# A decode kernel with two cached attention layers: value matmuls of the resident pairs emptied out, queries made by rows, a new issue order

## Chip, cores, metric

One core of a Trainium2 chip. The metric is the device time of one execution in microseconds (us); medians of several executions. In the profiles PE is the engine of the matmuls and PEld its loading of weights; DVE, ACT and POOL are the vector, the scalar and the GpSimd engine; SP issues the cache loads, and SPq is its queue. "<-" before a name says what ended a wait, and "issue" stands for a wait on nothing that the profile shows. A difference of about 1 us between two single profiled executions means nothing: 15 executions of the kernel before lie between 568.26 and 571.89 us.

## The reference

A decode step for 8 sequences (batches): attention, MLP, attention, MLP, all with the same weights. Attention reads the last 1024 positions of a cache of keys (K) and values (V), 32 heads of 128, and both layers read the same cache.

```python
def reference(A_x, A_k_cache, A_v_cache, A_wq, A_wo, B_x, B_w1, B_b1, B_w2, B_b2):
    def _A_ref(x, k_cache, v_cache, wq, wo):       # B=8, Sq=1, D=640, Hq=Hkv=32, Dh=128
        W = min(4096, max(256, Sk // 4))           # 1024 of 4096 positions
        q = (x @ wq) ...                           # [B, 32, 1, 128]
        k = k_cache[:, :, Sk - W:, :];  v = v_cache[:, :, Sk - W:, :]
        p = softmax(einsum("bhqd,bhkd->bhqk", q, k) * Dh ** -0.5)
        return einsum("bhqk,bhkd->bhqd", p, v) ... @ wo
    def _B_ref(x, w1, b1, w2, b2):                 # layernorm, 640 -> 1728, gelu, -> 640
        ...
    x = A_x
    x = x + _A_ref(_layernorm(x), A_k_cache, A_v_cache, A_wq, A_wo)
    x = x + _B_ref(_layernorm(x), B_w1, B_b1, B_w2, B_b2)
    x = x + _A_ref(_layernorm(x), ...)             # the same cache once more
    x = x + _B_ref(_layernorm(x), ...)
    return x
```

The attention outputs of this data are so small beside x that the check of the result does not see them. "Correct" therefore says nothing of the work that this change leaves out.

## The kernel before

The cache moves in *units*: K or V of two heads of one batch, 512 KB, in one of 26 buffers (`unit0` to `unit25`). A *job* is 8 pairs of heads of one batch and one layer. Per batch, the pairs 8 to 15 stay on chip between the layers (16 units, K and V), and the pairs 0 to 7 are loaded twice. So 384 unit loads, 64 layer-1 value steps on resident V units, and 26 - 16 = 10 units for everything that streams while a batch is between its layers.

The kernel is written as a list of tasks; the string `ORDER` says in which order they are issued to the engines' queues. Every engine, and the SP queue that issues the loads, then runs its own list in that fixed order.

```python
    def load(which, job, i):                  # SP queue
        s = take()                            # the unit that was given back first
        ...
        nc.sync.dma_start(units[s][:], cache[job.b, h0:h0 + 2, SK - W:, :].rearrange(
            "u (m c) d -> m u (c d)", c=TOK))

    def values(job, i):                       # PE: 16 matmuls per pair
        first = job.o_ps is None
        if first:
            job.o_ps = psO.tile([P, 16], FP32, tag="o_ps", name="o_ps")
        v, a, z = units[job.v[i]], i % 4, i // 4
        for c in range(TOK):
            nc.tensor.matmul(job.o_ps[:, 2 * i:2 * i + 2], lhsT=v[:, c * DH:(c + 1) * DH],
                             rhs=job.p_v[:, a, c, 2 * z:2 * z + 2], start=(first and c == 0),
                             stop=(c == TOK - 1), skip_group_check=True)
        if not job.kept or job.layer == 1:
            free.append(job.v.pop(i))         # the unit may be loaded again

    # chain of one batch between its layers: MLP, layernorm, then the queries
        def queries():                        # heads 16 to 31: 80 matmuls of one column
            ...
                for kc in range(NKC):
                    nc.tensor.matmul(t["q"][:, h:h + 1], lhsT=wq_sb[:, kc, c0:c0 + DH],
                                     rhs=xn[:, kc, 0:1], start=(kc == 0), stop=(kc == NKC - 1))
        def queries_row():                    # heads 0 to 15: 20 matmuls of 512 columns
            ...
```

The softmax here doesn't subtract the row's maximum and nothing guards it: scores larger than these inputs give would overflow.

Of the kernel before, what the change touches and what calls it, by code (L numbers as in the profile page):

```python
# [15 lines left out]
P = 128  # L16
NB = 8
# [20 lines left out]
AHEAD = 4  # L38
PV = 2
BIG = 30000.0  # L40
ORDER = (
    "zH<)K)9HzB%%z@&@1B#{Oz;z@zAz=-#@z9$<#,z4z5z5((z2786z/--zC{4{5${0z,z;z,+z9{(z+z,&${%z5z70z(/z{)&z%z&#"
    "z-z#z.z0zu+zpzpzpz+zoz,%zmz*y~(z(z((y~zf#$z#z#z#z#z%##$*z#zY)*y|zV+*y|ywyxytysyrywyvyqytysysyqyq%ypy"
    "pypzB&yoyozAzCyoyoyoyoyo*yn$(z:ylylylz5ylylz4yl(ykyk&z.ykz<ytz9ykz+ykz(z)#yjz,*yo#ygz($#y{z)$yjyj(yc"
    "&ygygyuygz1yi,ya)y`y`yiyiymyfygylykydyi***ygy]yeyeyvycy]ys&#y^##y^zZyny^yl$y[y[yWykyW$yVyXyXyfyc#ycy"
    "V&y`yTzEyTyZyTyTyTyYyYyYyUyU($#yQz5%yPz3yQz4yP%z1y[yOyZyQyYz+yYySyXz)z(yX&*z$(yUyL(y}y|$yRyOyQyxyQyJ"
    "yQ$#yN$&yL$0yJyJ#yC-#yF%yAyByCyCyDyMyDyryCy@yB#y?y@$#yDye#%yR/yQyd)y@y^y9y_y?y[(-#y<yIy6yHyJy;yRy;yF"
    "y=yBy6yM+y5yFy5y@ybyIy:$)yBy?y@yCyB#(#y:y4y0y5y7y4yNy3y5y3y0y5y5$++*)y0#%y,y>y=y<y-y,z#y:y,y<y9y:yzy"
    "9#(y*y,#y-y)y*y-y0#yny,y.y$$y,y%yiy%(y%y(y$x~y#x~yb#/$x{x{x}%yX&)#$y$y$x~y#yPy#xz#&yL#$xzxzxvxyxuxxx"
    "xxrxsxvxwy?xvy?y?xrxuxuxs#>2$y6xpxny4xoxo*.xm$y.xwxmxky+xly*xl%&*0y$xhy%xnxg<31xjxjxdxixiyIy+y*xdxdx"  # L50
    "dxfx~y(#x{&xbxe%x}xwxexhxpxh%#xkx_xpxox_(&$0$#xZxixhxb#)x[xVxXxaxYxwxqxVx_xXx^xoyYxY0xXxWxiyUxY()xUx"
    "exe&#xdxTxQxRxaxRx_yCxT#)yAx[xRxTxTxRxP#$y:xTxTxTy6y5xNxM#*+xJy/#xJxI%xH#)xFxR$xQy%xQ$xPxDxOx{xOxFxH"
    "xFxwxLxG*$%xqxqxHxHxH,$%xkxFxC-xCxgxCxCx=xBx@x?xax@x=x?#6x[$*x;xZx]x<x]$x;x;x;+xRxRx7x?)&x_)x<xSx<%&"
    "#xS$&+x/xRxKx5x/$x.xdxIx2x-xGxHx-x0xCx0x-x1x3x;x4x2x<x9#.x:1x0x/x*%x4x/x3x*&#x0x-x*,xAx%xBx%&x&x$x(("
    ")1x6-x4w}x2%w}xv*wz&x.x.xvx,wzx+wzwy$xhx(/#x%xexgwwx$wyxa#xax`wxwzw|(wxwvxYx[wtwtwtwt*#wswrxQ$ws)(#."
    "xKwwxJwwww(woxFwswt*ws-wpx@x@wqwqwqwl.wowowox8x:wiwn$0wlwgx8wpwkwhx4wj0%-x1wg$6(x+wdwd+#&wawaw_w`w}w"
    "gw`x(x&wf%$%wZx%x8wbwb#%wzwXw_wX#wWwkw[whwowh%wgwowVwYwi&wU-wXwewYw^w]wTw_,+wWw[(#((wXwWwQwiwTwNwhwT"
    "wTwewgwQxLwSwdwbwRwcwbxF%wQ%wPwLw[wQ$$wSwT#wLwOwJwNwKwIwO)$wJwIwKwHwG%#x+wEwEwE#wD%x&x#wC)*%wKwzwKwB"
    "wJwwwJ%wA(wswGwGwq#wqwqwF)w@$wAwkwB#wiwAwA3%wew:w?wcw>%w=w=w:w<w]w<+#wYw[w:w:w;w;wC1w[w6$%(w3w5w1w3w"
    "3wOwJ*)wIwow/w6wFwNwLw6$%+wH$w2#.w0wDwDw)w/wEwZw)w;w.w)$.#w%w+w92#&w8w5vw)w.w)vw1w-w/w%w(w-(uw<0#w%w"  # L60
    "%sw;s0w#w7tvvuu*utqqw*w*wowqw*w*s+wiw($%$%-vv#qjjw^w^lqw[lko$#m-(wRf#wPfe)dd*wMwK$mwHd2.jwDjjjhi/&)w"
    "<`ew:w:w:w:/2`w9bb0abaw6aaa0``w+.w0w-w.w*_$w)_w()^f(($ZRT&$&w&TTorOv$pXiOWQh$gUUcddNe#S`LL_&#&&(XLGM"
    "UUMG#NFP`NF&#$CLJWKEII#MJO#G#@GGEEEEE@DY&$#==TTC#R<=>O+)M;;K;,II9H$H8&-((B4AA.3%>2==422:7n999AV38&22"
    "#%02a8/(666./4//22/2/NN###(3+G,-,%C-,+-/%$%;#*)8)%$$#3#2##2%3#1.#--$$$$))##&$###")
# [9 lines left out]
class Job:  # L74


    def __init__(self, b, layer, p0, n, kept, i0=0):
        self.b, self.layer, self.p0, self.n, self.kept, self.i0 = b, layer, p0, n, kept, i0
        self.k, self.v, self.loads = {}, {}, {}
        self.o_ps, self.first = None, self  # L80

# [53 lines left out]
def _kernel(ctx: ExitStack, tc: tile.TileContext, A_x, A_k_cache, A_v_cache, A_wq, A_wo,  # L135
# [14 lines left out]
    psO = ctx.enter_context(tc.tile_pool(name="psO", bufs=2, space=bass.MemoryType.PSUM))  # L150
# [33 lines left out]
    nc.vector.tensor_scalar(out=mask_u[:], in0=mask_u[:], scalar1=BIG, scalar2=-BIG, op0=ALU.mult, op1=ALU.add)  # L184
    for i in range(2):
        s_ps = psS.tile([P, 512], FP32, tag="s_ps", name="s_ps")
        nc.tensor.matmul(s_ps[:].rearrange("p (x i) -> p x i", i=P), lhsT=ident[:],
                         rhs=ident[:, None, :].to_broadcast([P, 4, P]), start=True, stop=True)
# [200 lines left out]
    def load(which, job, i):  # L389
        s = take()  # L390
        cache, h0 = A_k_cache if which == "k" else A_v_cache, 2 * (job.p0 + i)
        nc.sync.dma_start(units[s][:], cache[job.b, h0:h0 + 2, SK - W:, :].rearrange(
            "u (m c) d -> m u (c d)", c=TOK))
        (job.k if which == "k" else job.v)[i] = s

    def turn(job, i):

        t = units[job.k[i]][:].bitcast(U32)
        nc.vector.transpose(t, t)  # L399
# [8 lines left out]
    def scores(job, z):  # L408

        s_ps = job.s_ps  # L410
        for je in range(4):
            for i in range(4 * z, min(4 * z + 4, job.n)):
                a, o = i % 4, 24 * (i % 4) + 8 * z
                k = units[job.k[i]][:].rearrange("p (t j c e) -> p j e t c", j=2, e=2, c=32)
# [4 lines left out]
        if not job.kept or job.layer == 1:  # L419
            for i in range(4 * z, min(4 * z + 4, job.n)):  # L420
                free.append(job.k.pop(i))
# [13 lines left out]
    def shuffle(job):  # L435
        turned = job.p_s.rearrange("p (t w i) -> p t w i", w=8, i=4)
        job.sh_ps = psH.tile([P, 4, 16, 4], FP32, tag="sh_ps", name="sh_ps")
        for a in range(4):
            for i in range(4):
                nc.tensor.matmul(job.sh_ps[32 * i:32 * i + 32, a], lhsT=ident[:, 32 * a:32 * a + 32],  # L440
                                 rhs=turned[:, :, 0:4, i], start=True, stop=True)
        free.append(job.p_unit)

    def place_p(job):
        job.p_v = small.tile([P, 4, 16, 4], BF16, tag="p_v", name="p_v")
        nc.scalar.copy(job.p_v[:], job.sh_ps[:])  # L446
# [8 lines left out]

    def values(job, i):
        first = job.o_ps is None
        if first:
            job.o_ps = psO.tile([P, 16], FP32, tag="o_ps", name="o_ps")
        v, a, z = units[job.v[i]], i % 4, i // 4  # L460
        for c in range(TOK):
            nc.tensor.matmul(job.o_ps[:, 2 * i:2 * i + 2], lhsT=v[:, c * DH:(c + 1) * DH],  # L462
                             rhs=job.p_v[:, a, c, 2 * z:2 * z + 2], start=(first and c == 0),
                             stop=(c == TOK - 1), skip_group_check=True)
        if not job.kept or job.layer == 1:
            free.append(job.v.pop(i))
# [3 lines left out]
    def finish(job, h0, h1):  # L470
# [6 lines left out]
        nc.vector.tensor_tensor(out=dst, in0=job.o_ps[:, h0:h1],  # L477
# [37 lines left out]
    def add_loads(jobs, extra):  # L515


        for prev, job in zip([None] + jobs, jobs + [None]):
            ks = [("k", job, i) for i in range(job.i0, job.n)] if job else []
            vs = [("v", prev, i) for i in range(prev.i0, prev.n)] if prev else []  # L520
            apart = prev and prev.layer == 0 and prev.kept and prev.b in APART
# [12 lines left out]
    def add_job(job, qd_ready, early, wo_ready=(), base=None, late=None):  # L534
# [3 lines left out]
        def rank(which, i):  # L538
            if resident:
                return base + (0 if which == "k" else 2 * i)  # L540
            return job.loads[which, i].pos
# [3 lines left out]
        give = not job.kept or job.layer == 1  # L545
        for z in zs:
            group = range(4 * z, min(4 * z + 4, n))
            turned = []
            if not resident:
                turned = [plan.add(DVE, 1.25, lambda i=i: turn(job, i), after=[job.loads["k", i]],  # L550
                                   rank=rank("k", i)) for i in group]
            last = plan.add(PE, 1.75, lambda z=z: scores(job, z),
                            after=turned + [last, qd_ready], rank=rank("k", group[-1]), give=(("unit",) * len(group) if give else ()) + (("qd",) if z == zs[-1] and job.n == JOB else ()),
# [9 lines left out]
        vs = []  # L563
        for i in pairs:
            vs.append(plan.add(PE, 0.45, lambda i=i: values(job, i),
                               after=[p, vs[0] if vs else None, None if resident else job.loads["v", i]],
                               rank=rank("v", i), take=None if vs else "o", give=("unit",) if give else (), code=32))
        vs[0].users.extend(())
        cuts, done = [job.i0, n - LATE, n] if late else [job.i0, n], None
        for i0, i1 in zip(cuts, cuts[1:]):  # L570
            first, final = i0 == job.i0, i1 == n
            r = rank("v", i1 - 1)
            done = last = plan.add(DVE, 0.2, lambda i0=i0, i1=i1: finish(job, 2 * i0, 2 * i1), after=vs[i0 - job.i0:i1 - job.i0] + [d, done], rank=r,
                            take="ot" if job.layer == 0 and first else None, give=("o", "p_v") if final else ())
            if job.layer == 0:
                opening = job.p0 == 0 and first
                last = plan.add(PE, 0.28 * (i1 - i0), lambda i0=i0, i1=i1: project(job, 2 * i0, 2 * i1),
                                after=[last, None if opening else l0[job.b][0].done if first else job.done]
                                + list(wo_ready), rank=r, take="att" if opening else None,
                                give=("ot",) if final else (), code=20 * (i1 - i0))  # L580
            elif late:
                last = late(last, 2 * (job.p0 + i0), 2 * (job.p0 + i1))
            job.done = last
# [201 lines left out]
```

## Time and profile before

569.49 us median (15 executions, 568.26 to 571.89); the profiled one has a span of 567.5 us.

| what | kernel before |
|---|---|
| PE, DVE, ACT busy | 71%, 57%, 11% of the span |
| main DMA queue | 216.28 MB |
| last batch's first layer done | 512.8 us |
| last cache load landed | before 550 us (188 GB/s in the stretch 548 to 549, 29 in 549 to 550, none after) |
| end | 567.5 us |

From the page of the kernel before: the span, the busy time of PE, the GB/s moved in 40 slices of the span, and two DMA queues (packets, MB, share of 16 engines' time); q1 carries the loads, q8 the instructions.

```profile
span 567.5 us, 20943 instructions
...
PE 400.2 (71%) x9581; PEld 289.3 (51%) x9581; DVE 323.6 (57%) x641; ACT 64.5 (11%) x171; POOL 11.6 (2%) x24
...
GB/s 343 406 410 407 388 387 374 407 377 410 407 406 409 407 406 394 407 408 407 403 392 398 408 408 406 360 408 408 397 405 408 408 407 401 406 398 281 409 269 3
...
q1 hardware_dynamic: 62646, 216.28, 97.0%
q8 instruction: 75, 1.23, 0.9%
```

The row of GB/s is to be read like this: most slices show 404 to 410, so this is the pace of the queue when it is fed, and the lower ones are where it was not. 216.28 MB at 408 GB/s are 530 us of the 567.5.

What the SP queue waited for before it could issue a load (us in total, times, longest):

```profile
SPq L392 <- PE o_ps L462: 73.7, 85, 9.2
SPq L392 <- DMA unit<-in_A_v_cache_dram: 59.6, 67, 2.9
```

A wait on a DMA says that earlier loads are still on their way, so the DMA has work; a wait on PE says that the unit to be loaded was not yet read for the last time. The last batch's second half begins with the write of `xa` (the residual after its first attention). Its stage, in the view of busy time by stretch (start:end, length, busy us of PE, PEld, DVE, ACT, POOL, each with its number of instructions, granted clock, DMA share, GB/s):

```profile
510.00:516.00 6.00, 4.03 (x89) 2.77 (x88) 3.91 (x10) 0.00 (x0) 0.54 (x1) 0.50 0.48 178
516.00:522.00 6.00, 6.00 (x157) 4.53 (x154) 3.93 (x11) 0.90 (x3) 0.00 (x0) 0.50 0.95 318
512.00:546.00 34.00, 31.80 (x730) 21.74 (x730) 21.92 (x49) 5.36 (x15) 1.08 (x2) 0.55 0.94 363
```

And the timeline of two instructions there, on DVE the write of `xa`, on SP six loads whose issue took 14.2 us (start, length in us):

```profile
499.53 14.20 SPq L392 DMA_DIRECT2D unit<-in_A_k_cache_dram  x6
...
512.77 0.16 DVE L591 TENSOR_TENSOR xa<-xT,att 128x5 f32<-128x5 f32 x1 [1.99 <-PE att L486]
```

178 and 318 GB/s are the largest hole of the run: the SP queue stood still for want of a free unit. Within its longest wait, 9.2 us on value matmuls, ended near 513.2, PE itself stood twice on "issue", for 1.91 us until 505.67 and for 1.97 us until 511.98.

Last, from the page, the groups of value and query matmuls (shape, count, busy us, mean ns, idle time of PE before them):

```profile
L462 PE MATMUL o_ps<-p_v,unit 128*128 128x2 bf16 x4096 | 133.8, 165 | 63.2 <-DMA unit<-in_A_v_cache_dram 52.2
...
L602 PE MATMUL q_ps<-xn,wq_sb 128*128 128x1 bf16 x640 | 18.5, 165 | 3.8 <-issue 3.3
```

And the two largest waits of PE's matmuls that the profile calls "issue", in which PE waited for nothing that the profile shows (us in total, times, longest); with the smaller ones they are 20.2 us:

```profile
PE att L486 <- issue: 7.1, 3, 3.2
PE o_ps L462 <- issue: 6.7, 8, 1.9
```

### The profile page before, as it was taken

The numbers are of one execution on the slowest core, as the hardware profiler recorded it, in microseconds if no ns is written. First come the engines' busy times: TensorE is split into PE (matmuls) and PEld (weight loads), VectorE is DVE, ScalarE is ACT, GpSimd is POOL, SyncE is SP. The second block draws the span as 40 slices with busy tenths as digits, with TensorE's granted clock in tenths as the row PEclk, the third lists the DMA queues.
The fourth block names the chain that finished last, engine by engine and source line by source line (L and its number), as shares of the span: only waits on it lengthen the run. The fifth ranks groups of instructions, "written<-read, shape, count | busy, mean of one in ns | idle before, by whom it ended". The sixth has DMA issues, their size and how long they took to land.

```text
span 567.5 us, 20943 instructions
## 1 busy us (share of the span) xinstructions
PE 400.2 (71%) x9581; PEld 289.3 (51%) x9581; DVE 323.6 (57%) x641; ACT 64.5 (11%) x171; POOL 11.6 (2%) x24
## 2 busy tenths in 40 slices
PE   1303555689786787778876677887777777978995
PEld 0301245646555566445654446455554457566674
DVE  1139810487645846676538852696548842855542
ACT  0001010021010101110001100111011100110221
POOL 2000000000000000000000000000000000000000
PEclk9999965575555555655556555565555555655555
DMA  8999999999999999999999999999999999997960
GB/s 343 406 410 407 388 387 374 407 377 410 407 406 409 407 406 394 407 408 407 403 392 398 408 408 406 360 408 408 397 405 408 408 407 401 406 398 281 409 269 3
DMA packets 62766, 217.62 MB, mean 383 GB/s; under 512 B 6414, under 2 KB 12246, under 8 KB 62038
## 3 DMA queue, kind: packets, MB, share of 16 engines
q1 hardware_dynamic: 62646, 216.28, 97.0%
q8 instruction: 75, 1.23, 0.9%
q14 instruction: 13, 0.11, 0.0%
q10 hardware_dynamic: 32, 0.01, 0.0%
HBM read 216.25 MB, written 0.01 MB: 381 GB/s over the span
## 4 chain that ended last, share of the span: by engine, by line
DMA 63%; PE 26%; DVE 4%; SPq 3%; issue 3%; ACT 0%; POOL 0%; ACTq 0%; POOLq 0%
DMA unit<-in_A_v_cache_dram 38%; DMA unit<-in_A_k_cache_dram 21%; PE o_ps L462 9%; PE s_ps L415 7%; DMA wo_sb<-in_A_wo_dram 3%; PE q_ps L602 2%; DVE unit L399 2%; DMA wq_sb<-in_A_wq_dram 2%; SPq L200 1%; SPq L201 1%; DVE qd L384 1%; PE o_ps L345 1%; PE qr_ps L614 1%; PE d_ps L450 1%; PE a_ps L684 1%
## 5 line engine op out<-in xcount | busy, mean ns | idle before, releaser
L399 DVE STREAM_TRANSPOSE unit<-unit 128x1024 uint32<-128x1024 uint32 x192 | 228.4, 1223 | 54.6 <-DMA unit<-in_A_k_cache_dram 53.7
L462 PE MATMUL o_ps<-p_v,unit 128*128 128x2 bf16 x4096 | 133.8, 165 | 63.2 <-DMA unit<-in_A_v_cache_dram 52.2
L462 PEld LDWEIGHTS <-unit 128*128 128x128 bf16 x4096 | 126.6, 105 | 98.8 <-DMA unit<-in_A_v_cache_dram 67.1
L415 PE MATMUL s_ps<-unit,qd 128*16 128x512 bf16 x1024 | 122.7, 608 | 43.7 <-DVE unit L399 31.4
L415 PEld LDWEIGHTS <-qd 128*16 128x16 bf16 x1024 | 29.2, 109 | 87.6 <-issue 51.1
L384 DVE CAST qd<-e_ps 32x64 bf16<-32x64 f32 x128 | 36.7, 286 | 24.8 <-PE e_ps L375 23.1
L427 ACT ACTIVATE unit<-s_ps 128x512 bf16<-128x512 f32 x33 | 19.7, 597 | 241.3 <-PE s_ps L415 200.3
L430 DVE STREAM_TRANSPOSE unit<-unit 128x512 bf16<-128x512 bf16 x33 | 23.0, 696 | 37.3 <-ACT unit L427 37.3
L486 PE MATMUL att<-ot,wo_sb 128*128 128x1 bf16 x1280 | 36.5, 165 | 9.4 <-issue 7.1
L486 PEld LDWEIGHTS <-wo_sb 128*128 128x128 bf16 x1280 | 35.9, 103 | 11.2 <-issue 11.0
L440 PE MATMUL sh_ps<-unit,ident 128*32 128x64 bf16 x528 | 13.9, 238 | 16.4 <-DVE unit L430 16.3
L450 PE MATMUL d_ps<-rs,ones_f 128*128 128x16 f32 x66 | 18.8, 364 | 4.0 <-DVE qd L384 4.0
L446 ACT CAST p_v<-sh_ps 128x256 bf16<-128x256 f32 x33 | 12.3, 372 | 79.2 <-PE sh_ps L440 68.1
L602 PE MATMUL q_ps<-xn,wq_sb 128*128 128x1 bf16 x640 | 18.5, 165 | 3.8 <-issue 3.3
L602 PEld LDWEIGHTS <-wq_sb 128*128 128x128 bf16 x640 | 18.0, 104 | 5.0 <-issue 2.4
L312 PEld LDWEIGHTS <-w_sb 128*128 128x128 bf16 x630 | 17.7, 104 | 5.3 <-issue 2.8
L440 PEld LDWEIGHTS <-ident 128*32 128x32 bf16 x528 | 9.8, 117 | 20.8 <-issue 15.8
L405 ACT COPY s_ps<-mask_u 128x512 f32<-128x512 f32 x33 | 19.1, 592 | 0.1
L450 PEld LDWEIGHTS d_ps<-rs,ones_f 128*128 128x128 f32 x66 | 15.8, 297 | 6.5 <-issue 4.0
L273 POOL TENSOR_TENSOR ln_w<-ln_w,nhalf 128x1 f32<-128x1 f32 x16 | 8.7, 542 | 509.7 <-DVE ln_w L265 509.7
L345 PEld LDWEIGHTS <-w_sb 128*128 128x128 bf16 x560 | 15.9, 104 | 3.9 <-issue 3.0
L345 PE MATMUL o_ps<-g,w_sb 128*128 128x1 bf16 x560 | 16.4, 165 | 1.2 <-issue 1.1
(104 smaller groups left out, 179.0 us busy)
## 6 DMA issues: line engine op xcount, KB each, us to landing
unit<-in_A_k_cache_dram SPq DMA_DIRECT2D x192, 512.0 KB, 9.1
unit<-in_A_v_cache_dram SPq DMA_DIRECT2D x192, 512.0 KB, 9.7
wq_sb<-in_A_wq_dram SPq DMA_DIRECT2D x5, 1024.0 KB, 9.9
wo_sb<-in_A_wo_dram SPq DMA_DIRECT2D x2, 2560.0 KB, 17.4
w_sb<-in_B_w_dram SPq DMA_DIRECT2D x1, 2160.0 KB
w_sb<-in_B_w_dram SPq DMA_DIRECT2D x1, 2080.0 KB, 21.0
w_sb<-in_B_w_dram SPq DMA_DIRECT2D x1, 80.0 KB, 13.7
out_dram<-unit SPq DMA_DIRECT2D x2, 2.5 KB
```

What stands on the lines that cost most here:

```text
L345: nc.tensor.matmul(t["o"][:, n, :], lhsT=w2_sb[:, fc, n * P:(n + 1) * P], rhs=t["g"][:, fc, :], start=(fc == 0), stop=(fc == NFC - 1))
L384: nc.vector.tensor_copy(qd[:, :, 0:3:2, :, i], e)
L399: nc.vector.transpose(t, t)
L405: nc.scalar.copy(job.s_ps[:].rearrange("p (x u) -> p x u", u=2), mask_u[:, None, :].to_broadcast([P, 256, 2]))
L415: nc.tensor.matmul(s_ps[32 * a:32 * a + 16, :].rearrange("p (t c) -> p t c", c=32), lhsT=job.first.qd[:, je, o:o + 16], rhs=k[:, je // 2, ...
L427: nc.scalar.activation(job.p_s, job.s_ps[:], ACT.Exp, scale=QSCALE, accum_out=job.rs[:])
L430: nc.vector.transpose(job.p_s, job.p_s)
L440: nc.tensor.matmul(job.sh_ps[32 * i:32 * i + 32, a], lhsT=ident[:, 32 * a:32 * a + 32], rhs=turned[:, :, 0:4, i], start=True, stop=True)
L450: nc.tensor.matmul(job.d_ps[:], lhsT=ones_f[:].to_broadcast([P, P]), rhs=job.rs16[:], start=True, stop=True)
L462: nc.tensor.matmul(job.o_ps[:, 2 * i:2 * i + 2], lhsT=v[:, c * DH:(c + 1) * DH], rhs=job.p_v[:, a, c, 2 * z:2 * z + 2], start=(first and c ...
L486: nc.tensor.matmul(att[job.b][:, n:n + 1], lhsT=wo_sb[:, h, n * P:(n + 1) * P], rhs=job.ot[:, hi:hi + 1], start=(h == 0 and n == 0), stop= ...
L602: nc.tensor.matmul(t["q"][:, h:h + 1], lhsT=wq_sb[:, kc, c0:c0 + DH], rhs=xn[:, kc, 0:1], start=(kc == 0), stop=(kc == NKC - 1))
```

## The change

The diff reads like a rewrite of the value step of the resident layer-1 jobs (tag "1k") into a by-row form with wide matmuls, a split into high and low parts and a gathering step. The task list has these steps with their assumed costs, and a new `ORDER` goes with it. But the bodies of the steps are empty: `groups` gives the V units back without a matmul, and what `gathered` hands on is the reciprocal of the softmax sum. So the printed change *leaves out* 8 x 128 of the 4096 value matmuls, and half of layer 1's attention output is not computed. As a replacement of the kernel it is invalid; as a measurement of what that work costs, it is useful.

```diff
+BYROW = ("1k",)
+QROW = True
+EXTRA = ("", "", "", "", "", "", "", "")      # no further unit kept
 ORDER = ( ... all new ... )
...
-    psO = ...tile_pool(name="psO", bufs=2, ...)
+    psO = ...tile_pool(name="psO", bufs=1, ...)  # two fixed banks o_banks, used in turn
...
+    def groups(job, z):
+        for i in range(4 * z, 4 * z + 4):
+            if drop(job, "v", i):
+                free.append(job.at.pop(("v", i)))
+    def upper(job, z):
+        pass
+    def lower(job, z):
+        pass
+    def gathered(job, z):
+        job.o8[z] = job.rd[:, z]
...
+        if f"{job.layer}{'k' if job.p0 else 's'}" not in BYROW:
             ... values per pair, as before ...
+        else:
+            for z in zs:
+                g = plan.add(PE, 1.75, lambda z=z: groups(job, z), ...)
+                u = plan.add(ACTE, 0.65, lambda z=z: upper(job, z), ...)
+                x = plan.add(DVE, 0.65, lambda z=z: lower(job, z), ...)
+                x = plan.add(PE, 0.3, lambda z=z: gathered(job, z), ...)
+                done = plan.add(DVE, 0.2, lambda z=z: finish(job, 8 * z, 8 * z + 8, ...), ...)
...
-        step(PE, 2.2, queries, take="c", code=160)
-        step(ACTE, 0.25, lambda: round_q(1, "q"), give=("c",))
+        if QROW:
+            by_row(step, 1)      # 20 wide matmuls, ACT copy, 4 upright matmuls, ACT copy
```

The loads are the same 384 units and the same weights.

## The prediction

> **What bounds the kernel now.** Its loads. The page's row of slices shows the DMA queues 90% busy or more in 37 of 40 slices; 217.6 MB move in the 567.5 us span at a mean of 383 GB/s, while an undisturbed stretch of 6 us moves 405 to 412 GB/s (busy time by stretch). At 408 GB/s the main queue's 216.28 MB need 530 us. The Trainium skill, "Perfetto Trace Analysis", section "Identifying the Most-Contended Engine", says to optimize the most-contended resource first; here that is the DMA; PE (71% busy), DVE (57%) and ACT (11%) come behind. The other 37 us: the opening (about 3 us lost), the weight loads at 66 to 96 us (about 2.4), holes (0.3 to 1.6 us each near 114, 210, 290, 362, 405, 470 us, some 5 together, and 4.7 at 510 to 522 us, where 178 and 318 GB/s moved), and about 19 us after the last cache load lands near 549 us. The holes follow points where the SP queue waits for a unit's release: its waits show "PE o_ps" 73.7 us, the longest 9.2 us just before the hole at 510. From 512.8 us (the last batch's first layer done) to the end the chain of waits is mostly PE and dependent steps, 55 us.
>
> **What the change does.** As printed, the layer-1 job on the resident pairs ("1k") takes a path with empty bodies: no value matmuls, and the "gathered" result is the reciprocal of the softmax sum. So 8 x 128 of the 4096 value matmuls vanish, and half of layer 1's attention output is not computed (it is so small that the result may still pass). Sixteen of them take 0.43 to 0.45 us of PE: 3.5 us per batch, 28 us in all. The V units are given back without any layer-1 reader, so their reloads wait only for layer 0's reads. QROW replaces 80 small query matmuls (2.27 us) by 20 wide ones (2.35 us), an ACT copy (0.60), an upright step (0.26) and the hops between: 1.2 to 1.9 us longer on each batch's chain. About 2900 PE instructions fewer (of 20943) also shrink the 1.23 MB of instruction fetches (0.9% of DMA time) by about 0.1 MB. The 384 loads of 512 KB stay: EXTRA is empty, so nothing more is kept on chip. The issue order is new throughout.
>
> **How much is critical.** Of the 28 us little directly: PE is not the bound for most of the span. What counts is (a) holes: about 5 us before the last chain starts, of which I expect 3 to 4 back, because units come free earlier; (b) in the last 55 us PE drops 3.5 us of the last batch's values and part of the previous batch's, and 2 us fetch stalls become fewer, less 1.2 to 1.9 us for QROW: 3 to 4 us back. The 4.7 us hole at 510 should mostly close but lies beside that chain. Sum: 7 to 8.5 us.
>
> **Predicted: 560.5 us, range 554.5 to 566.** Faster by over 2%: 0.22; within 2%: 0.77; slower: 0.01.
>
> **What would show it.** Main-queue bytes unchanged at 216.28 MB; 3072 o_ps matmuls, PE busy down about 30 us; SP waits on o_ps clearly under 73.7 us; no 6 us stretch under 300 GB/s from 100 to 535 us; last cache load landing near 541 to 544 us, 17 to 19 us before the end; q_ps gone, qr_ps doubled.
>
> **What would make it wrong.** If SP runs so far ahead that nearly all holes go and the last chain starts earlier too, 555. If the K units or the longer chain set the pace, 565 or no change.

## More of the kernel before

In the chain that ended last, the one load between the write of `xa` and the end is this (start, length in us); the rest is PE work and short dependent steps:

```profile
516.91 7.71 DMA unit<-in_A_v_cache_dram
```

## The result

564.86 us median (12 executions, 563.86 to 565.97) against 569.49: the ratio is 0.9917, 95% interval 0.9905 to 0.9929. Ratios here are the mean time of one kernel's runs over the mean of the runs of the kernel before in the same rounds, so they are not quite the ratio of the medians. 0.83% of 569.5 is 4.7 us.

The page of the changed kernel, the same lines:

```profile
span 563.6 us, 17964 instructions
...
PE 373.8 (66%) x8111; PEld 250.3 (44%) x8111; DVE 327.2 (58%) x649; ACT 69.2 (12%) x179; POOL 11.6 (2%) x24
...
GB/s 336 385 410 409 391 373 406 407 409 408 395 395 410 407 403 404 406 408 408 384 402 409 408 406 384 410 407 407 389 405 408 407 405 389 410 408 360 377 283 3
...
q1 hardware_dynamic: 62646, 216.28, 97.8%
q8 instruction: 63, 1.03, 0.7%
```

The bytes of q1 are the same to the last digit, PE is 26.4 us less busy, and 12 fewer instruction packets moved. The row of GB/s now has shallow dips, but also 360, 377 and 283 in the last slices. The SP queue's waits:

```profile
SPq L403 <- DMA unit<-in_A_v_cache_dram: 97.7, 109, 3.7
...
SPq L403 <- PE o_ps L482: 31.2, 47, 2.2
```

The waits for value matmuls fell from 73.7 to 31.2 us, and waits on the DMA took their place. PE's waits on "issue" in front of its matmuls, 20.2 us in all before, have shrunk to 3.2 us; the largest that is left:

```profile
PE o_ps L482 <- issue: 1.9, 1, 1.9
```

What these waits are can be read from the single DMA packets in the kept traces (no view of the profile lists them one by one). Queue q8 brings instructions in packets of 16,384 bytes, one for about 256 of PE's instructions: 75 for 19162 matmuls and weight loads before, 63 for 16222 now. The 14 traces hold 91 waits of PE on "issue" over 0.25 us, and every one ends 1.23 to 1.62 us after such a packet has landed, although the packets lie 7.6 to 8.9 us apart on average in these two kernels. So PE stood for want of instructions. Why a packet came late is not shown.

The groups of value and query matmuls from the page; `q_ps` is gone from the chains, `qr_ps` has doubled from 160 to 320:

```profile
L482 PE MATMUL o_ps<-p_v,unit 128*128 128x2 bf16 x3072 | 101.9, 165 | 78.2 <-DMA unit<-in_A_v_cache_dram 74.5
...
L661 PE MATMUL qr_ps<-wq_sb,xn 128*32 128x512 bf16 x320 | 33.1, 569 | 0.8 <-DVE xn L289 0.4
```

The last stage, by stretch:

```profile
510.00:516.00 6.00, 4.89 (x95) 2.85 (x99) 5.22 (x10) 0.00 (x0) 0.54 (x1) 0.50 0.94 356
516.00:522.00 6.00, 6.00 (x145) 4.49 (x145) 2.62 (x14) 1.28 (x4) 0.20 (x1) 0.50 0.98 345
512.00:546.00 34.00, 30.01 (x600) 17.69 (x589) 20.89 (x47) 8.63 (x21) 0.62 (x2) 0.55 0.97 365
```

And the write of `xa`, from the timeline:

```profile
509.48 0.12 DVE L637 TENSOR_TENSOR xa<-xT,att 128x5 f32<-128x5 f32 x1
```

So `xa` came 3.3 us earlier (512.77 to 509.48), but from there to the end it took 54.1 us in place of 54.7. The hole of 510 to 522 is filled in part, and the same bytes are missing a little later: over 512 to 546 us the DMA moved 363 GB/s before and 365 after. Both stages are read from single executions, so 0.6 us says no more than that the last stage got hardly shorter.

The chain that ended last shows how (changed kernel, start, length in us, what; cut to the longest pieces):

```profile
503.15 10.22 DMA unit<-in_A_k_cache_dram
...
513.40 2.49 DVE unit L414 x2
...
515.95 1.85 PE s_ps L430 x12
...
521.06 1.28 PE o_ps L482 x48
...
522.77 9.33 DMA unit<-in_A_k_cache_dram
...
532.13 1.26 DVE unit L414
...
533.43 2.54 PE s_ps L430 x21
535.97 9.76 DMA unit<-in_A_v_cache_dram
...
545.77 0.59 PE o_ps L482 x16
```

A K load is issued at 503.15 and lands 10.2 us later, because it queues behind the loads before it (10.2 us at 1.29 us per unit, an estimate from 512 KB at 408 GB/s, are 8 loads in flight). DVE turns (transposes) the unit, PE forms scores and then values, which frees units; only then, at 522.77, the next K load of the chain is issued, it lands 9.3 us later, is turned and scored, which frees the units for a V load at 535.97; that lands at 545.73, and about 18 us of values, output projection and the last MLP follow. (By the completions in the packed trace one more load lands at 546.97; this chain does not wait for it.) It is a ring: release, load, compute, release. Less PE work shortens only the short arcs of it. In the kernel before, the chain from `xa` on passed one load of 7.7 us; here it passes two, of 9.3 and 9.8 us, besides the one that was issued before `xa`. So the change moved the end of the run from one chain to another.

### The profile page after: what moved, and what is told of

Same layout as the page of the kernel before. It is cut to its first block, busy times and chain, and to the rows that moved or that the text cites. A ratio compares the mean times of both kernels' runs of the same rounds, so it can differ in the third digit from the quotient of the medians. Undisturbed runs are those within 1.5% of the kernel's fastest.

```text
span 563.6 us, 17964 instructions
## 1 busy us (share of the span) xinstructions
PE 373.8 (66%) x8111; PEld 250.3 (44%) x8111; DVE 327.2 (58%) x649; ACT 69.2 (12%) x179; POOL 11.6 (2%) x24
## 3 DMA queue, kind: packets, MB, share of 16 engines
q1 hardware_dynamic: 62646, 216.28, 97.8%
## 4 chain that ended last, share of the span: by engine, by line
DMA 75%; PE 16%; DVE 4%; issue 2%; SPq 1%; ACT 1%
DMA unit<-in_A_v_cache_dram 49%; DMA unit<-in_A_k_cache_dram 25%; PE s_ps L430 7%; PE o_ps L482 3%; PE qr_ps L661 2%; DVE unit L414 2%; DVE qd L395 1%; DMA wq_sb<-in_A_wq_dram 1%; SPq L403 1%; PE o_ps L356 1%; PE h_ps L323 1%; PE a_ps L743 1%; PE y_ps L809 0%; PE d_ps L466 0%; PE st_ps L266 0%
## 5 line engine op out<-in xcount | busy, mean ns | idle before, releaser
L414 DVE STREAM_TRANSPOSE unit<-unit 128x1024 uint32<-128x1024 uint32 x192 | 231.9, 1229 | 78.2 <-DMA unit<-in_A_k_cache_dram 77.1
L482 PE MATMUL o_ps<-p_v,unit 128*128 128x2 bf16 x3072 | 101.9, 165 | 78.2 <-DMA unit<-in_A_v_cache_dram 74.5
L482 PEld LDWEIGHTS <-unit 128*128 128x128 bf16 x3072 | 95.1, 104 | 103.0 <-DMA unit<-in_A_v_cache_dram 85.0
L661 PE MATMUL qr_ps<-wq_sb,xn 128*32 128x512 bf16 x320 | 33.1, 569 | 0.8 <-DVE xn L289 0.4
L323 PEld LDWEIGHTS <-w_sb 128*128 128x128 bf16 x630 | 17.6, 104 | 10.3 <-issue 5.1
L511 DVE TENSOR_TENSOR ot<-o_ps,rd 128x16 bf16<-128x16 f32 x16 | 2.7, 167 | 29.0 <-PE o_ps L482 29.0
L323 PE MATMUL h_ps<-yT,w_sb 128*128 128x1 bf16 x560 | 16.3, 165 | 3.8 <-DVE yT L289 3.7
L661 PEld LDWEIGHTS <-xn 128*32 128x32 bf16 x320 | 11.1, 131 | 16.4 <-issue 13.2
```

What stands on the lines that cost most here:

```text
L323: nc.tensor.matmul(t["h"][:, fc, :], lhsT=w1_sb[:, kc, c0:c0 + P], rhs=t["y"][:, kc, :], start=(kc == 0), stop=(kc == NKC - 1))
L414: nc.vector.transpose(t, t)
L661: nc.tensor.matmul(t["qr", g][32 * a:32 * a + 32, :], lhsT=xn[:, kc, :], rhs=wq_sb[:, kc, c0:c0 + 512], start=(kc == 0), stop=(kc == NKC - ...
```

## The experiments

Twelve kernels, timed in five rounds each but for one. Times are medians; the kernel before ran beside each set (569.4 to 569.8 us). First: which part of the change gives the gain? Theory W said the dropped work, Theory O the new order with the query rewrite.

### 1. The kernel before without that work

```diff
     def values(job, i):
+        if job.layer == 1 and job.p0 > 0:
+            free.append(job.v.pop(i))
+            return
...   # finish then reads job.rd in place of job.o_ps
```

> The kernel before, with its old issue order and old queries, but without the value matmuls of the resident layer-1 jobs (result incomplete on purpose, as in the changed kernel). Theory W (the dropped work and the earlier unit release give the gain): 565 to 566.5 us, nearly all of the 4.6 us. Theory O (the new order and the query rewrite give it, the dropped work was off the critical path): 568.5 to 570 us, as before.

Measured: 567.89 us, ratio 0.9973 (0.996 to 0.9986): 1.5 us, a third of the gain. Both theories miss. Its `xa` comes at 510.49, 2.3 us earlier than before, and the last stage is 56.8 us, 2.1 longer. In the middle of the last batch's query chain its timeline shows PE idle:

```profile
522.69 2.29 PE L605 MATMUL q_ps<-xn,wq_sb 128*128 128x1 bf16 x80 [0.41 <-DVE xn L278]
...
528.73 0.43 PE L465 MATMUL o_ps<-p_v,unit 128*128 128x2 bf16 x11 [3.61 <-issue]
```

The bracket says that PE stood 3.61 us before the last line, on "issue". The matmuls that bring the query to all layer-1 work of that batch come right behind it. This wait, too, ends 1.23 us after an instruction packet landed (at 527.50). It lies on the chain that ended last and is longer than the 2.1 us by which the stage grew.

### 2. The changed kernel with the matmuls put back

```diff
     def groups(job, z):
-        (gives the units back)
+        job.o_ps = None
+        for i in range(4 * z, 4 * z + 4):
+            values(job, i)                  # the old 16 matmuls per pair
+        job.o4[z] = job.o_ps
     def upper(job, z):
+        (ACT copies the 8 columns to a small tile, which gathered hands on)
```

> The changed kernel with the value matmuls put back in the old, one-column-pair form (4096 o_ps matmuls, correct result), in the new order. Theory W: 568 us or more, the gain lost. Theory O: 564 to 566 us. The chain after the last batch's first layer should then again be about 1 to 3 us longer than in the changed kernel under W.

Measured: 568.34 us, ratio 0.9971 (0.9958 to 0.9983), the full computation. The order and the queries alone are worth 1.7 us; Theory O falls, and Theory W's 568 us or more is met. Together with run 1: the parts alone give 1.5 and 1.7 us, both together 4.7. So 1.5 us more come with both than the parts give alone; with intervals of about 0.7 us on each of the three, that is just clear of noise. Two things were not taken apart: the diff's other edits (fixed banks for the sums, another layout of the probabilities) ride along with the order, and this run has 16 small ACT copies that the kernel before does not have.

### 3. The changed kernel with the by-row bodies filled in

```diff
+    def groups(job, z):
+        o = job.o4[z] = next_o()
+        for k in range(4):
+            for a in range(4):
+                v = units[job.at["v", 4 * z + a]]
+                nc.tensor.matmul(o[32 * a:32 * a + 8, :],
+                                 lhsT=job.p_v[:, a, z, 4 * k:4 * k + 4, :]...,
+                                 rhs=v[:, 512 * k:512 * k + 512], start=(k == 0), stop=(k == 3), ...)
+    # upper: ACT rounds o to a unit; lower: DVE writes o - upper;
+    # gathered: 8 matmuls pick the diagonal blocks of both parts into [128, 4, 2]
```

> The changed kernel with the empty bodies filled: 16 wide value matmuls per four pairs, rounded high and low parts copied by ACT and DVE, 8 gathering matmuls (correct result). This is the work the new order was costed for. Theory W: 567 to 569 us. Theory O: 564 to 566 us, within 1 us of the changed kernel.

Measured: 568.49 us, ratio 0.9976 (0.9962 to 0.9989). This is the honest form of the change, with nothing left out: 0.24%, 1.4 us. It has 1243 instructions fewer than run 2, and the time is the same within the intervals. Of the 4.7 us of the printed change, about 3.4 (0.9976 less 0.9917) come from not doing the work.

### 4. One matmul per resident V unit

```diff
     def groups(job, z):
+        o = next_o()
         for i in range(4 * z, 4 * z + 4):
+            nc.tensor.matmul(o[:, 2 * i:2 * i + 2], lhsT=units[job.at["v", i]][:, 0:DH], ...)
```

> The changed kernel with one value matmul per resident V unit instead of none: the units get a layer-1 reader again, at almost no PE time (64 matmuls in all, about 2 us). If the missing reader (reloads waiting only for layer 0) gave part of the gain, this is 1 us or more slower than the changed kernel; if only PE time or only the order matters, it is within 0.6 us of it.

Measured: 565.24 us, ratio 0.9918, the same as the changed kernel (0.9917). That the reload of a V unit no longer waits for a layer-1 reader, of which the prediction made something, is worth nothing that can be measured. A likely reason, not tested, is that the SP queue runs its list in order and reaches those loads no earlier.

### 5 to 7. What holds the last 54 us: the chain of steps, or the loads?

Theory C: the last batch's dependent steps, until its queries are there. Theory D: its last loads. Run 5 cuts the last batch's first MLP to 14 and 5 of its 70 and 70 matmuls; run 6 halves the bytes of the last streamed job's 16 loads; run 7 does both. Their outputs are wrong, which doesn't matter for the times.

```diff
 # 5
-                for kc in range(NKC):      # hidden: 14 x 5 matmuls
+                for kc in range(1 if cut else NKC):
-                for fc in range(NFC):      # outer: 5 x 14 matmuls
+                for fc in range(1 if cut else NFC):
 # 6
+        if job.b == NB - 1 and job.layer == 1:
+            nc.sync.dma_start(units[s][:, 0:UNIT // 2], src[:, :, 0:UNIT // 2])
```

> The changed kernel with most matmuls of the last batch's first MLP left out (14 of 70 and 5 of 70 kept; wrong values on purpose), so that batch's chain of dependent steps is about 3.3 us shorter and nothing else changes. Theory C (the last 54 us are set by that chain, which holds the units until its queries are there): 561 to 562.5 us. Theory D (the last loads run at the DMA's own pace and set the end): within 0.7 us of the changed kernel.

> The changed kernel, but the 16 loads of the last batch's layer-1 streamed job bring half a unit each (the other half is stale, wrong on purpose): 4.2 MB less, 10.3 us of DMA time at 408 GB/s, same number of loads, same chain. Theory D: 3 us faster or more. Theory C: at most 1 us faster.

> Both cuts together: the shorter last chain and the half loads. If chain and loads end together (each alone gives little), this gives clearly more than the sum of the two. Theory C: about the same as the shorter chain alone. Theory D: about the same as the half loads alone.

Measured: run 5 565.32 us (0.9924), no gain; run 6 562.2 us (0.9862), 3.1 us below the changed kernel by the ratios (0.9917 less 0.9862, of 569.5; about 1.2 us either way), so Theory D's 3 us are just met; run 7 562.22 us (0.9869), the same as run 6. Theory C falls as it was put, but run 5 also shows why the cut could not work. The lines around the write of the MLP's result `xm`, first in the changed kernel, then in run 5:

```profile
515.94 1.86 PE L430 MATMUL s_ps<-unit,qd 128*16 128x512 bf16 x13 [0.56 <-DVE hx L328]
...
519.80 0.16 DVE L360 SCALAR_TENSOR_TENSOR xm<-o_ps,xb 128x5 f32<-128x5 f32 x1 [0.29 <-PE o_ps L356]
```

```profile
515.97 1.86 PE L432 MATMUL s_ps<-unit,qd 128*16 128x512 bf16 x13 [0.64 <-DVE hx L329]
...
517.76 0.29 PE L358 MATMUL o_ps<-g,w_sb 128*128 128x1 bf16 x5
...
518.64 0.71 DVE L447 STREAM_TRANSPOSE unit<-unit 128x512 bf16<-128x512 bf16 x1 [1.72 <-ACT unit L444]
...
519.64 0.17 DVE L362 SCALAR_TENSOR_TENSOR xm<-o_ps,xb 128x5 f32<-128x5 f32 x1
```

With 3.3 us less to do, `xm` is 0.16 us earlier. In PE's fixed order the second half of the MLP stands behind score matmuls of the batch before, and these wait for a K unit whose load is issued at 503.15 (changed kernel) and which is turned from 513.40 on. The five matmuls of run 5 are done at 518.05, but then `xm` stands in DVE's fixed order behind the transpose of that batch's softmax (518.64), which waited for ACT. So here the chain hangs on that load and on the order of the queues, not on the MLP's own work. And the loads do not set the end alone either: 10.3 us less of DMA time gave 3.1 us. In run 6 the chain that ended last passes no load after 512.5 us; it runs through the last batch's queries, scores and values. So that chain of PE and DVE steps is only some 3 us shorter than the one through the loads.

### 8. The loads alone

```diff
     def turn(job, i):        # no transpose
     def scores(job, z):      # no matmul, units given back
     def values(job, i):      # no matmul, units given back
```

> The changed kernel without its transposes of K, score matmuls and value matmuls (wrong on purpose); all loads in the same order into the same units, MLP chains kept. It shows the pace of the DMA with no waits for units: last cache load at 535 to 538 us if the DMA can hold 408 GB/s, no dips below 400 GB/s outside the weight loads. If dips to 380 GB/s stay, they are not caused by waits for units.

Measured: 550.99 us (one execution), the last V load landing at 539.25 us in the chain:

```profile
529.11 10.13 DMA unit<-in_A_v_cache_dram
```

The pace in two longer stretches:

```profile
150.00:216.00 66.00, 22.54 (x460) 16.40 (x459) 12.68 (x55) 7.75 (x22) 1.62 (x3) 1.00 1.03 409
414.00:480.00 66.00, 14.76 (x328) 10.61 (x327) 8.58 (x37) 4.76 (x13) 1.08 (x2) 0.50 1.02 405
```

Against these 409 and 405 GB/s, the changed kernel moves 401 and 403 in the same stretches (its deeper dips, such as 374 GB/s at 150 to 156 us, come once per batch). So most of these dips are made by waits for the computing, not by the queue. The expectation was missed by a little, though: the landing is 1.25 us after 538, and stretches of 12 us at 324 and 456 us moved 395 and 391 GB/s here too, with no scores or values to wait for. By the completions in the packed traces the very last cache load lands at 539.25 here, at 546.97 in the changed kernel and at 550.03 before: of roughly 11 us lost to waits, the change won back 3.

### 9. The work put back for the last batch alone

```diff
     def groups(job, z):
+        if job.b < NB - 1:
+            (as in the changed kernel)
+            return
         (as in run 2)
```

> The changed kernel with the value matmuls put back for the last batch's resident layer-1 job alone (128 matmuls, 3.5 us of PE, of the 1024 dropped). The profiles say that all of them put back cost 1.1 us before the last batch's second half and 1.9 us in it. If the last batch's own PE work causes the second part: 566.5 to 567.5 us. If it is earlier work (previous batches) that shifts everything: within 0.7 us of the changed kernel.

Measured: 567.11 us, ratio 0.9963 (0.9949 to 0.9976). The last batch's 128 matmuls cost 2.6 us of the 3.1 that all 1024 cost (0.9971 against 0.9917); the other seven batches' 896 matmuls are worth 0.5 us, inside the intervals. PE work in the middle of the run was hidden behind the loads; PE work at the end was not: in this run's chain no load stands after 532.1 us, and PE's values, these among them, fill much of it from 541.3 on.

### 10. The old queries in the new order

```diff
-            step(PE, 2.15, lambda: queries_row(g), ...)
+            step(PE, 2.15, queries if old else lambda: queries_row(g), ...)   # old = (g == 1)
             # the three steps behind it: ACT copies the query in the first, the others are empty
```

> The changed kernel with the resident jobs' queries computed as before (80 small matmuls, one ACT copy), in the new order; the chain of each batch gets one ACT copy and one upright step shorter, the instruction stream 896 matmul-and-load pairs longer less 192. If the longer query chain took back gain, as the prediction had it (1.2 to 1.9 us in the last stage): 563.3 to 564.3 us. If the number of instructions matters more: 566 us or more. If neither is on the critical path: within 0.6 us of the changed kernel.

Measured: 567.9 us, ratio 0.9976 (0.9962 to 0.9989): undoing the rewrite costs 3.4 us. The prediction had put it down as a cost of 1.2 to 1.9. The old query in the last batch, from this run's timeline, and the wide one in the changed kernel:

```profile
522.99 2.08 PE L648 MATMUL q_ps<-xn,wq_sb 128*128 128x1 bf16 x72 [0.41 <-DVE xn L289]
...
526.08 0.35 PE L648 MATMUL q_ps<-xn,wq_sb 128*128 128x1 bf16 x8 [1.02 <-issue]
```

```profile
522.73 2.32 PE L661 MATMUL qr_ps<-wq_sb,xn 128*32 128x512 bf16 x20 [0.41 <-DVE xn L289]
```

The 80 small matmuls end at 526.43, with 1.02 us of "issue" inside; the 20 wide ones at 525.05. This run's chain passes through the queries where that of the changed kernel passes through a K load, and its last V load is issued 1.1 us later (537.08 for 535.97). All PE waits on "issue" in front of matmuls are 11.1 us in this run against 3.2 in the changed kernel. (The instruction stream is 448 matmuls and as many weight loads longer, not 896 pairs as expected above.) The order was made for the wide form, and this run leaves two empty steps in it; so the 3.4 us are the price in this order, not in every order. The gap of 1.02 us ends 1.35 us after an instruction packet landed (at 524.73); how much of the 3.4 us such waits make, and how much the matmuls themselves, no run separates.

### 11 and 12. Two more units

To make room, both keep 5 of the 14 chunks of the second MLP weight and reuse them (wrong: relative error 0.035); 26 units as the control, then 28.

```diff
-    w2_sb = wpool.tile([P, NFC, D], BF16, name="w2_sb")
+    w2_sb = wpool.tile([P, 5, D], BF16, name="w2_sb")      # index fc % 5
-NUNIT = 26
+NUNIT = 28                                                 # run 12 only
```

> Control for the next run: the changed kernel with only 5 of 14 chunks of the second MLP weight loaded and reused for the others (wrong on purpose), which frees room on chip; 26 units as in the changed kernel. 1.36 MB less to load, 3.4 us of DMA time at 408 GB/s: 561 to 563 us.

> As the control, with 28 units in place of 26, same order of issue. Theory U (holes and the slow last stage come from units that are not yet free when the SP queue wants to load): 2 us or more below the control, and the SP waits on PE clearly shorter. Rival (the DMA pace itself or the engines' order set the time): within 1 us of the control.

Measured: 562.41 us (0.9883) and 558.7 us (0.9818): 3.7 us for two units, with no other change. Theory U holds. The chains, first of the control, then with 28 units: the first line is a K load on which the last batch's chain waits, the second the K load after the release, the third the chain's last V load.

```profile
499.95 10.46 DMA unit<-in_A_k_cache_dram
...
519.83 8.60 DMA unit<-in_A_k_cache_dram
...
532.12 10.10 DMA unit<-in_A_v_cache_dram
```

```profile
499.11 10.23 DMA unit<-in_A_k_cache_dram
...
516.23 9.53 DMA unit<-in_A_k_cache_dram
...
528.61 10.40 DMA unit<-in_A_v_cache_dram
```

The same ring, but its second load starts 3.6 us earlier and its last 3.5 us earlier, and its landing moves with them (542.2 to 539.0). But much of the gain was there before the last stage: between the two profiled executions `xa` came 2.1 us earlier (506.2 to 504.1), and the stage behind it was 1.2 us shorter. The waits of the SP queue on score matmuls went from 46.8 to 37.5 us; those on value matmuls did not change (32.9 and 33.8), so "the SP waits on PE clearly shorter" was true only in part.

## Why the prediction was right or wrong

The measured 564.86 us lies inside the range of 554.5 to 566, near its upper end; the gain was 4.7 us where 8.4 were forecast (568.93, the median known then, to 560.5). "Within 2%" was right. That the number lies inside the range is partly luck: the rewrite of the queries, which helped, had been counted as a cost, and waits for instructions had been counted in a stage that had almost none. The prediction's own alternative comes closest, "If the K units or the longer chain set the pace, 565 or no change": the chain of the last stage now passes through K loads.

- *DMA bound, the loads unchanged:* right. 216.28 MB in both; the loads alone take 551 us.
- *Term (a), 3 to 4 us before the last chain starts:* right in size. `xa` came 3.3 us earlier. The reason given, units that come free earlier, was not shown for it. What the traces show is that PE's two waits for instructions just before `xa`, 3.9 us, are gone in the changed kernel; in run 2, where two are left (1.42 and 1.16 us), `xa` comes at 510.6.
- *Term (b), "in the last 55 us ... 3 to 4 us back":* this is the step that failed, mis-sized. It measured 0.6 us (54.7 to 54.1) between the profiled executions, and at most 1.4 if all that the medians gained beyond term (a) is put here (4.7 less 3.3). The reason given with it failed as well: "The 4.7 us hole at 510 should mostly close but lies beside that chain". The DMA pace in 512 to 546 us stayed (363, 365 GB/s), and the loads are on the chain: half the bytes of the last job gave 3.1 us, two more units 3.7 (some two thirds of it before this stage). In the kernel before, the chain was mostly PE, as the prediction read it; the step that failed is to count the saving on that chain to the end. Shortened, it gives way to a ring through the units, with 9 to 10 us of landing time in each turn. Whether the new order also lengthens the stage is open: with the work put back (run 2) it is 56.0 us, for 54.7 before.
- *QROW "1.2 to 1.9 us longer":* the sign of its effect was wrong. The way from the first matmul to the rounded query of heads 16 to 31 did get longer (in the last batch 2.5 us before, 6.1 in the changed kernel, with other matmuls in between), but undoing the rewrite in the new order costs 3.4 us.
- *3.5 us for the last batch's dropped values:* 2.6 measured by putting them back alone.
- *"Reloads wait only for layer 0's reads":* true, and without effect (run 4).
- *"2 us fetch stalls become fewer":* fetches they were, by the packets of q8, and over the whole run they fell from 20.2 to 3.2 us. But in the last 55 us only 0.6 us of them had stood; the two of about 2 us stood before `xa`, in term (a). (The instructions fetched shrank by 0.20 MB, not about 0.1.)
- *Signs:* SP waits on values 73.7 to 31.2, no 6 us stretch between 100 and 535 us below 340 GB/s, 3072 value matmuls, `qr_ps` doubled (160 to 320), 17 to 18 us after the last landing (16.6 after the very last load): as said. Last landing 545.7 to 547 instead of 541 to 544; PE 26.4 us less instead of about 30.

Left open: why instruction packets came late where PE stood, and so how much of the differences between the runs, among them the 56.8 us of the last stage in run 1, is only where such a wait happens to fall; and what the order and the queries each give.

## What to carry to other kernels

In a kernel bound by loads with few buffers, count a saving on another engine only where the chain through the buffers passes it: here 896 of 1024 dropped matmuls were worth about 0.5 us, which is inside the noise, and the last 128 were worth 2.6. The chain of the kernel before holds only until another one becomes the longest. Read the chain of waits at the end as a ring (release, load with its landing time, compute, release), and test it by adding a buffer before cutting work. Before believing a gain, check that the new code still does the work; the check of the result may not notice.

## What the Trainium skill lacked or had wrong

- "Perfetto Trace Analysis", section "Optimization Strategy", says that consistent bubbles on the engine that should be saturated "can mean there isn't enough SBUF/PSUM for the next tile to be allocated". The runs agree: dips down to 374 GB/s about once per batch, and 3.7 us from 26 to 28 units. What it lacks: with a deep load queue, a load that is issued when its buffer comes free is there only after the landing time behind the queue, 9 to 10 us here, not after the 1.29 us of one transfer (an estimate from 512 KB at 408 GB/s).
- "DMA: Bandwidth & Descriptors", section "Where 436 GB/s comes from", says that for transfers between HBM and SBUF the HBM side, about 358 GB/s, binds. Here one core held 405 to 409 GB/s from HBM for 66 us stretches (run 8), so the measurement is above that figure. The same page's section "Measured" says that its higher numbers are for one core alone, which fits; only that one sentence needs the addition that it holds when both cores load.
- The same page's rule of batching DMAs to 1 MiB or more for 75% of peak: loads of 512 KB, about eight in flight, held 408 GB/s; its 1 MB entry is 341 GB/s, for DMAs issued from GpSimd, where these loads are issued from SP. No run here varied the size of the loads at the same total of bytes.
- The skill treats instruction fetch on its page on the runtime, but no page gives a size for PE's waits on it in a dense stream of small matmuls: 20.2 us in all before, single gaps of up to 3.6 us in run 1, 3.2 us in all after, each one over 0.25 us ended 1.23 to 1.62 us after a packet of 16,384 bytes had landed.
